# Batch 0's state products are stored and loaded ahead of the other batches', and one product changes place at the end of each pair

## The chip, the cores and the metric

The kernel runs on one core of one Trainium2 chip. The metric is the device time of one execution in microseconds (us), the median of several runs. Before the change it is 1326.22 us over 3 runs (1325.0 to 1326.81). Inside the core, TensorE (PE) multiplies matrices, VectorE (DVE), ScalarE (ACT) and GpSimd (POOL) work on elements, and SyncE (SP) issues most of the transfers between the on-chip memory and the chip's large memory (DRAM).

## The reference

Inputs are float32 or float64 arrays that the kernel takes as raw words where they are 64 bits wide. Three blocks follow one another:

```python
# attention: x is [8, 8, 512, 64], state is [8, 8, 32, 64] (batch, head, row, 64)
a     = softmax(x @ state.T / 8);   xread = a  @ state
a2    = softmax(state @ x.T / 8);   sread = a2 @ x
x     = concat([xread, sread], rows)              # per batch 512 + 32 rows
x     = x.transpose(0, 2, 1, 3).reshape(8 * 544, 512)

# block 1: w1, w2 [512, 1024], w3 [1024, 1024], w_out [1024, 512]
x     = ((x @ w1) * (x @ w2)) @ w3 @ w_out

# block 2: w_a, w_b [512, 1536], w_out [1536, 512]
out   = ((x @ w_a) * (x @ w_b)) @ w_out           # [4352, 512]
```

## The kernel before, in words

**How the work is arranged.** Every float32 product is made of three matrix multiplications on a high and a low part of each operand (`PASSES`, high x high, high x low, low x high). Block 1 does not form xread: since xread = a @ state, the kernel multiplies the state by w1 and w2 first. That gives one *state product* per batch, 256 rows by 2048 columns, and block 1 for the 512 x-rows of a batch is then (a @ product).

**The opening, up to about 180 us**, does four things at once: it converts and splits the weights, forms w3 @ w_out (tiles `wp`, then `ws`), runs the attention of batches 0 and 1, and makes the state products. A state product is made for four batches together: `state_product(p, nh, bg, i)` (L317) multiplies the state of head pair p of batches 4·bg to 4·bg+3 by half i of the column half nh of the weights `wk{p}_{nh}`. Two heads r give two PSUM banks `pb`. ACT or DVE copies them (`product_move`, L331) to a tile `sg{p}_{nh}_{bg}_{r}`, whose 128 rows are 4 batches by 32 state rows. `product_store` (L340) then writes the four 32-row parts to four DRAM buffers `p_d0` to `p_d3` (or `p_d4` to `p_d7` for bg = 1), one transfer each. There are 16 such tiles for each bg.

Before batch 0 can be multiplied, `load_p` (L597) loads its product back in four column chunks `pr0_0` to `pr0_3`, each over all rows. Chunks 0 and 1 need the stores with nh = 0, chunks 2 and 3 those with nh = 1. ACT casts a chunk to its high part `ph`, POOL subtracts to get the low part `pl` (`split`, L145 and L151). Two row chunks f of block 1 read one column chunk: `first_product` (L1107, its matmuls are at L1119, tiles `f0_*` and `f1_*`, 24 matmuls for the two f of a chunk), after which ACT and DVE make `fh`. When all eight `fh` exist, `first_output` (L1349, tiles `x2f0` to `x2f3`, 24 matmuls each) multiplies by `ws`. Batch 1 and the following batches run in a plain loop with tiles `ap`, `bp` and `x2p`.

**What sets the order of the opening.** Each piece of work is a `Job` with an engine, a planned duration, its predecessors (`after`), the number of free on-chip tiles it needs (`need`, plus `keep` that must stay free), a priority number and a `lag` after its predecessors. `run_jobs` (L724) always takes the job that could start first by its own clock, with the priority as a small handicap, or, among transfers, as the tie-breaker. What it picks becomes the order of instructions on each engine, and every engine then runs its own list strictly in this order. SP's list holds the stores and the loads together. The store of a tile is one job for all four batches, with priority `len(loads) + STORE_BEHIND`. The products of bg = 1 are jobs of low priority between the others.

**Block 2** works on pairs of batches g = 0 to 3 (`block2`, L1679) with a seven-product scheme in place of eight. For each row chunk f = 0 to 11 it does S2·T2 (into `r`, copied to `e2`), A12·B21 (into `q`), S4·B22 (added into `v`), S3·T3 (added into `r`), then the first two products of chunk f + 1, and then A22·T4 (added into `r`, L1756). Before A22·T4 may add into `r`, DVE must have added `r` into `e5` (`add`, L1583). For the last chunk, f = 11, there is no chunk f + 1, and A22·T4 stands directly behind S3·T3. After the twelve chunks, the results are multiplied by w_out (tiles `ro`, `vo`, `qo`).

Of the kernel before, what the change touches and what calls it, by code (L numbers as in the profile page):

```python
# [32 lines left out]
KEEP = 9  # L33
KEEP_SG = 2
KEEP_UNTIL = 40
STORE_BEHIND = 18

LATE_KEEP = 6
LATE_PRIO = 10
# [21 lines left out]
MARGIN = 1.5  # L61

P_AHEAD = 3
X_SLOT = 0
PASSES = ((0, 0), (0, 1), (1, 0))

# [2 lines left out]
def attention_moe_moe2(  # L69
# [18 lines left out]
    B, H, S, D = x.shape  # L88
# [10 lines left out]
    NF2 = DFF2 // P  # L99
# [16 lines left out]
    def charge(**work):  # L116
        for e, t in work.items():
            through[e] = max(through[e], now[0]) + t
        return max(through[e] for e in work)
# [43 lines left out]
    class Convert:  # L163
# [25 lines left out]
        def add(self, i):  # L189
            d, out = self.words(i)[1], self.out[:, i * 512 : (i + 1) * 512].bitcast(I32)  # L190
            nc.gpsimd.tensor_tensor(out=out, in0=out, in1=d.bitcast(I32), op=ALU.add)
            free(self.raws[i][0])
# [144 lines left out]
        else:  # L337
            nc.vector.tensor_copy(dst, src)

    def product_store(p, nh, bg, r):  # L340
        for j in range(4):
            nc.sync.dma_start(
                out=p_d[4 * bg + j][r, p, :, nh * 1024 : (nh + 1) * 1024],
                in_=sg[p, nh, bg, r][j * NS : (j + 1) * NS],
            )
# [330 lines left out]
    loads = []  # L676
# [53 lines left out]
            )  # L730
        return lows

    stores = {0: [], 1: []}

    def early_wk(p, nh):
        adds = convert_jobs(f"wk{p}_{nh}")
        last = []
        for bg in range(1):
            moves = {0: [], 1: []}
            for i in range(2):  # L740
                pr = Job(
                    "P",
                    1.0,
                    lambda a=(p, nh, bg, i): state_product(*a),
                    after=[adds[i], state_moved[bg]] + last[-1:],
                    need=2 - 2 * i,
                    keep=KEEP_SG,
                    prio=2 + len(loads) / 100,
                    banks=("ps", 2),
                )  # L750
                last.append(pr)
                for r in range(2):
                    moves[r].append(
                        Job(
                            "AV",
                            (0.6, 0.85),
                            lambda e, a=(p, nh, bg, i, r): product_move(*a, e),
                            after=[pr],
                            prio=0,
                        ).gives("ps", 1)  # L760
                    )
            for r in range(2):
                st = Job(
                    "D",
                    1.5,
                    lambda a=(p, nh, bg, r): product_store(*a),
                    after=moves[r],
                    prio=len(loads) + STORE_BEHIND,
                    lag=2.0,
                ).frees(f"sg{p}_{nh}_{bg}_{r}")  # L770
                if bg == 0:
                    stores[nh].append(st)
        return last

    def frees_after(after, *names):
# [47 lines left out]
    for name in EARLY:  # L823
        if name[:2] == "wk":
            p, nh = int(name[2]), int(name[4])
# [6 lines left out]
        elif name[:2] == "w3":  # L832
# [3 lines left out]
            for k in range(2):  # L836
# [4 lines left out]
                    after=list(adds),  # L841
                    prio=0,
# [6 lines left out]
                    after=[tr] + lows,  # L849
# [530 lines left out]
    for b, qs in ((0, range(4)), (1, range(3))):  # L1380
        for q in qs:
            l = Job(
                "D",
                1.5,
                lambda b=b, q=q: load_p(b, q),
                after=stores[q // 2] + ([last] if last else []),
                need=1,
                prio=1 + 20 * b,
                lag=1.0,
            )  # L1390
            if b == 0 or q == 0:
                sp = Job("A", 1.1, lambda b=b, q=q: split_p(b, q), after=[l], need=2, prio=0 + 5 * b)
                ready[b, q] = last = Job("G", 2.4, nothing, after=[sp], prio=0 + 5 * b)
    lows = []
    mults = []
    for f in range(NF1):
# [168 lines left out]
    def product(t, g, f, block, x, first):  # L1565
        for k in range(2):
            w = weights(g, f, block, k)
            for i, (m, q) in enumerate(PASSES):
                nc.tensor.matmul(  # L1569
                    t,  # L1570
                    lhsT=w[m],
                    rhs=xf[g].parts[x][q][:, k, :],
                    start=first and k == 0 and i == 0,
                    stop=k == 1 and i == 2,
                    skip_group_check=True,
                )
        now[0] += 6 * 512 / 2400 * 1.0625
# [101 lines left out]
    def block2(g):  # L1679
# [35 lines left out]
        def reload(f, i):  # L1715
            if g:
                free(f"w{g}_{f}_{i}")
                if f + 2 < NF2:
                    load_w(g, f + 2, [i])
# [4 lines left out]
        for f in range(NF2):  # L1724
# [7 lines left out]
            charge(A=0.6)  # L1732
            more()
            q = bank(f"q{name}")
            product(q, g, f, A12, "B21", True)
            reload(f, 1)
            add(e1, e1, q)
            charge(V=0.7)
            more()
            product(v, g, f, S4, "B22", False)  # L1740
            add(e2, e2, v)
            charge(V=0.7)
# [8 lines left out]
            h = [flat(out2.raw[f"{i + 1}{half}", j][1], S)[:, c, :] for i in range(2)]  # L1751
            nc.gpsimd.tensor_tensor(out=h[1], in0=e2, in1=e5, op=ALU.mult)  # L1752
            charge(G=1.3)
            if f + 1 < NF2:
                begin(f + 1)
            more()  # L1756
            product(r, g, f, A22, "T4", False)
            nc.vector.tensor_tensor(out=h[0], in0=e1, in1=r, op=ALU.mult)  # L1758
# [196 lines left out]
```

## Time and profile before

| | |
|---|---|
| median of 3 runs | 1326.22 us (1325.0 to 1326.81) |
| the profiled execution, its own time | 1323.77 us |
| span of the profile | 1322.0 us |
| PE busy | 1281.9 us, 97% of the span |
| DVE / ACT / POOL busy | 57% / 44% / 44% |
| granted TensorE clock, mean | 0.988 of full speed |

The profiled execution took 1323.77 us, 1.8 us more than its span; it is 2.45 us quicker than the median. PE is busy nearly all of the time, so a change shows in the end time mainly through what it does to the moments in which PE has nothing to do or runs at a lower clock. Busy shares of the other engines say little here: an idle engine that PE does not wait for costs nothing. Times in the rows count from the start of the span.

### The profile page before, as it was taken

Reading aid. Unit: us, or ns where it says so; the run is one execution under the profiler, and the core shown is the slowest. Engines: PE = TensorE matmul, PEld = TensorE weight load, DVE = VectorE, ACT = ScalarE, POOL = GpSimd, SP = SyncE. Lnnn points to the kernel's source line nnn. Section 1 sums busy time; section 2 is a strip of 40 time slices with the busy share of each in tenths; the row PEclk is TensorE's granted clock in tenths of the full one; section 3 lists DMA queues with packets and bytes.
Section 4 is the critical chain, followed back from the end, with each engine's and each line's share of the span. In section 5 each row is a group of like instructions: output and inputs, shape, how many; then the busy total and the mean of one; then the engine's idle time right before and its main releaser. Section 6 shows DMA issues by size and latency. Waiting matters only on the chain.

```text
span 1322.0 us, 19779 instructions
## 1 busy us (share of the span) xinstructions
PE 1281.9 (97%) x7514; PEld 1081.5 (82%) x7514; DVE 750.2 (57%) x861; ACT 585.5 (44%) x956; POOL 588.0 (44%) x398
## 2 busy tenths in 40 slices
PE   6996999999999999999999999999999999999998
PEld 4763778777777788888888998889988889988798
DVE  5883316557567566565665962247922359533493
ACT  7894535655565666545432431123511225212232
POOL 5671314563546567456447541147311264212460
PEclk7997999999999999999999999999999999999999
DMA  9988754762677561789584779316695247873271
GB/s 310 291 253 261 223 154 130 243 176 80 213 234 219 178 208 33 252 291 294 190 316 140 250 244 387 128 27 237 221 408 183 64 159 263 330 271 108 80 254 65
DMA packets 155134, 276.56 MB, mean 209 GB/s; under 512 B 47136, under 2 KB 92192, under 8 KB 155040
## 3 DMA queue, kind: packets, MB, share of 16 engines
q1 hardware_dynamic: 150752, 260.09, 59.5%
q0 software_dynamic: 4288, 15.21, 2.9%
q8 instruction: 60, 0.98, 0.3%
q14 instruction: 34, 0.28, 0.1%
HBM read 205.00 MB, written 70.25 MB: 208 GB/s over the span
## 4 chain that ended last, share of the span: by engine, by line
PE 86%; DMA 4%; DVE 3%; issue 2%; ACT 2%; SPq 1%; POOL 1%; POOLq 0%; ACTq 0%; DVEq 0%
PE r L1569 19%; PE ro L1887 10%; PE x2p L1178 10%; PE v L1569 9%; PE vo L1887 5%; PE bp L1119 5%; PE ap L1119 5%; PE q L1569 5%; PE qo L1887 3%; PE abs L1652 2%; PE f L1119 2%; PE x2f L1356 2%; PE wp L368 2%; PE srv L1826 1%; PE pb L324 1%
## 5 line engine op out<-in xcount | busy, mean ns | idle before, releaser
L1752 POOL TENSOR_TENSOR r<-e,e 128x512 f32<-128x512 f32 x48 | 63.5, 1324 | 283.9 <-DVE e L1583 283.9
L1178 PE MATMUL x2p<-hp,ws 128*128 128x512 f32 x672 | 162.0, 390 | 0.0
L151 POOL TENSOR_TENSOR pl<-pr,ph 128x512 fp32r<-128x512 f32 x64 | 87.4, 1385 | 137.3 <-ACT ph L145 104.8
L1178 PEld LDWEIGHTS x2p<-hp,ws 128*128 128x128 f32 x672 | 125.7, 188 | 26.3
L1703 ACT COPY e<-r 128x512 f32<-128x512 f32 x48 | 28.2, 588 | 188.7 <-PE r L1569 188.6
L1758 DVE TENSOR_TENSOR r<-e,r 128x512 f32<-128x512 f32 x48 | 33.0, 687 | 133.2 <-PE r L1569 133.2
L1143 DVE TENSOR_TENSOR hfp<-asbp,bp 128x512 f32<-128x512 f32 x56 | 38.3, 684 | 77.8 <-PE bp L1119 77.1
L151 DVE TENSOR_TENSOR hp<-hfp,hp 128x512 fp32r<-128x512 f32 x56 | 56.4, 1008 | 40.1 <-ACT hp L145 40.1
L1583 DVE TENSOR_TENSOR e<-e,q 128x512 f32<-128x512 f32 x48 | 32.9, 685 | 78.8 <-PE q L1569 78.8
L1607 POOL TENSOR_TENSOR r<-r,r 128x1024 f32<-128x1024 f32 x24 | 71.8, 3008 | 0.9
L1569 PE MATMUL r<-xT4h,w 128*128 128x512 f32 x192 | 67.8, 393 | 4.3 <-DVE e L1583 4.3
L1569 PE MATMUL r<-xT3h,w 128*128 128x512 f32 x192 | 67.1, 390 | 0.8 <-ACT e L1731 0.8
L1569 PE MATMUL r<-xT2h,w 128*128 128x512 f32 x192 | 67.1, 390 | 0.0
L1569 PE MATMUL r<-xB11h,w 128*128 128x512 f32 x192 | 67.0, 389 | 0.0
L1569 PE MATMUL q<-xB21h,w 128*128 128x512 f32 x192 | 66.9, 389 | 0.0
L1569 PE MATMUL v<-xB22h,w 128*128 128x512 f32 x192 | 66.9, 389 | 0.0
L1569 PE MATMUL v<-xT1h,w 128*128 128x512 f32 x192 | 66.9, 389 | 0.0
L145 ACT CAST hp<-hfp 128x512 fp32r<-128x512 f32 x56 | 34.8, 621 | 64.1 <-DVE hfp L1143 63.7
L1731 ACT COPY e<-r 128x512 f32<-128x512 f32 x48 | 28.3, 589 | 70.8 <-PE r L1569 70.8
L1137 ACT COPY asbp<-ap 128x512 f32<-128x512 f32 x56 | 32.8, 586 | 51.3 <-PE ap L1119 51.1
L1119 PE MATMUL bp<-ah,ph 128*128 128x512 f32 x112 | 48.0, 429 | 0.2 <-DVE hfp L1143 0.2
L1569 PEld LDWEIGHTS r<-xT4h,w 128*128 128x128 f32 x192 | 36.0, 188 | 14.6 <-DVE e L1583 7.2
(503 smaller groups left out, 3830.1 us busy)
## 6 DMA issues: line engine op xcount, KB each, us to landing
w<-w_d SPq DMA_DIRECT2D x132, 512.0 KB, 7.6
zz<-z_d SPq DMA_DIRECT2D x84, 512.0 KB, 4.5
w_d<-w SPq DMA_DIRECT2D x96, 256.0 KB, 3.2
p_d<-sg SPq DMA_DIRECT2D x128, 128.0 KB, 2.5
pr<-p_d SPq DMA_DIRECT2D x32, 512.0 KB, 5.8
w<-w_d SPq DMA_DIRECT2D x36, 256.0 KB, 8.4
x<-in_x_dram SPq DMA_DIRECT2D x64, 128.0 KB, 5.1
sw<-in_moe_w_dram SPq DMA_DIRECT2D x16, 512.0 KB, 5.2
```

What stands on the lines that cost most here:

```text
L145: nc.scalar.copy(hi, src)
L151: (eng or nc.vector).tensor_tensor(out=lo[:, i], in0=src[:, i], in1=hi[:, i].bitcast(F32), op=ALU.subtract)
L1119: nc.tensor.matmul(dst[:, :n], lhsT=l[m], rhs=r[q], start=i == 0 and j == 0, stop=i == k - 1 and j == 2,)
L1137: nc.scalar.copy(a_sb[:, :n], pa[:, :n])
L1143: nc.vector.tensor_tensor(out=hf[:, :n], in0=a_sb[:, :n], in1=pb[:, :n], op=ALU.mult)
L1178: nc.tensor.matmul(acc[j], lhsT=w_s[f][:, m, j * P : (j + 1) * P], rhs=h[:, q, :n], start=per == 1 and f == 0 and i == 0, stop=f == NF1 - ...
L1569: nc.tensor.matmul(t, lhsT=w[m], rhs=xf[g].parts[x][q][:, k, :], start=first and k == 0 and i == 0, stop=k == 1 and i == 2, skip_group_che ...
L1583: nc.vector.tensor_tensor(out=out, in0=x, in1=y, op=ALU.add)
L1607: ENGINES[eng].tensor_tensor(out=out, in0=x, in1=y, op=op)
L1752: nc.gpsimd.tensor_tensor(out=h[1], in0=e2, in1=e5, op=ALU.mult)
L1758: nc.vector.tensor_tensor(out=h[0], in0=e1, in1=r, op=ALU.mult)
L1887: nc.tensor.matmul(dst, lhsT=hl[m][:, k, i * P : (i + 1) * P], rhs=z[:, k, q, :], start=FIRST[p] and j == 0 and k == 0 and i % 2 == 0 and ...
```

## The change

It has two parts that do not touch each other.

**Stores and loads of batch 0.** The store of a bg = 0 tile is split in two jobs: the part of batch 0 with priority `len(loads) + STORE_FIRST` (6), and the parts of batches 1 to 3 behind it with `len(loads) + STORE_BEHIND` (now 40, before 18). The stores of bg = 1 stay one job each, with the latter priority. The loads of batch 0 wait for the first kind alone, the loads of batch 1 for the second. The loads of batch 0 are chained to one another, no longer to the split of the chunk before; they leave three tiles free (`P_KEEP`), and their planned lag grows from 1 to 4 us. The number of transfers, their sizes and all arithmetic stay as they were.

**The last row chunk of a pair.** For f = 11, A12·B21 with its addition on DVE moves from between S2·T2 and S4·B22 to between S3·T3 and A22·T4.

```diff
-STORE_BEHIND = 18
+STORE_FIRST = 6
+STORE_BEHIND = 40
...
+P_KEEP = 3
...
-    def product_store(p, nh, bg, r):
-        for j in range(4):
+    def product_store(p, nh, bg, r, js=range(4)):
+        for j in js:
             nc.sync.dma_start(
                 out=p_d[4 * bg + j][r, p, :, nh * 1024 : (nh + 1) * 1024],
                 in_=sg[p, nh, bg, r][j * NS : (j + 1) * NS],
...
-    stores = {0: [], 1: []}
+    stores = {(b, nh): [] for b in range(2) for nh in range(2)}
...
             for r in range(2):
                 st = Job(
                     "D",
+                    0.5,
+                    lambda a=(p, nh, bg, r, (0,)): product_store(*a),
+                    after=moves[r],
+                    prio=len(loads) + STORE_FIRST,
+                    lag=2.6,
+                )
+                rest = Job(
+                    "D",
                     1.5,
-                    lambda a=(p, nh, bg, r): product_store(*a),
-                    after=moves[r],
+                    lambda a=(p, nh, bg, r, (1, 2, 3)): product_store(*a),
+                    after=[*moves[r], st],
                     prio=len(loads) + STORE_BEHIND,
-                    lag=2.0,
+                    lag=2.6,
                 ).frees(f"sg{p}_{nh}_{bg}_{r}")
-                if bg == 0:
-                    stores[nh].append(st)
+                stores[0, nh].append(st)
+                stores[1, nh].append(rest)
...
                 lambda b=b, q=q: load_p(b, q),
-                after=stores[q // 2] + ([last] if last else []),
+                after=stores[b, q // 2] + ([last] if last else []),
                 need=1,
+                keep=P_KEEP,
                 prio=1 + 20 * b,
-                lag=1.0,
-            )
+                lag=4.0,
+            )
+            last = l if b == 0 else last
             if b == 0 or q == 0:
                 sp = Job("A", 1.1, lambda b=b, q=q: split_p(b, q), after=[l], need=2, prio=0 + 5 * b)
-                ready[b, q] = last = Job("G", 2.4, nothing, after=[sp], prio=0 + 5 * b)
+                ready[b, q] = Job("G", 2.4, nothing, after=[sp], prio=0 + 5 * b)
+            if q == (3, 0)[b]:
+                last = ready[b, q]
...
             q = bank(f"q{name}")
-            product(q, g, f, A12, "B21", True)
-            reload(f, 1)
-            add(e1, e1, q)
-            charge(V=0.7)
-            more()
+
+            def inner():
+                product(q, g, f, A12, "B21", True)
+                reload(f, 1)
+                add(e1, e1, q)
+                charge(V=0.7)
+                more()
+
+            last = f == NF2 - 1
+            if not last:
+                inner()
             product(v, g, f, S4, "B22", False)
...
-            if f + 1 < NF2:
+            if not last:
                 begin(f + 1)
+            else:
+                inner()
             more()
             product(r, g, f, A22, "T4", False)
```

**What moves on SP.** The stores of a tile end in its tile name and the batch is the number behind `p_d`; `pr0_0` is batch 0's first chunk. Around its load, before the change (56 stores stand ahead of the load):

```order
L342 DMA p_d2_85<-sg0_1_0_0_1037 32x1024
L342 DMA p_d3_86<-sg0_1_0_0_1037 32x1024
L342 DMA p_d0_83<-sg0_1_0_1_1040 32x1024
L342 DMA p_d1_84<-sg0_1_0_1_1040 32x1024
L342 DMA p_d2_85<-sg0_1_0_1_1040 32x1024
L342 DMA p_d3_86<-sg0_1_0_1_1040 32x1024
L600 DMA pr0_0_1204<-p_d0_83 128x2x512
L342 DMA p_d0_83<-sg3_1_0_0_1068 32x1024
```

And after it, on the same engine:

```order
L344 DMA p_d0_83<-sg2_0_0_0_1018 32x1024
L344 DMA p_d0_83<-sg2_0_0_1_1021 32x1024
L344 DMA p_d0_83<-sg0_1_0_0_1025 32x1024
L344 DMA p_d0_83<-sg0_1_0_1_1028 32x1024
L344 DMA p_d1_84<-sg0_0_0_1_942 32x1024
L344 DMA p_d2_85<-sg0_0_0_1_942 32x1024
L344 DMA p_d3_86<-sg0_0_0_1_942 32x1024
L344 DMA p_d1_84<-sg1_1_0_0_949 32x1024
L344 DMA p_d2_85<-sg1_1_0_0_949 32x1024
L344 DMA p_d3_86<-sg1_1_0_0_949 32x1024
L602 DMA pr0_0_1123<-p_d0_83 128x2x512
L344 DMA p_d0_83<-sg3_1_0_0_1055 32x1024
```

Now 29 stores stand ahead of the load: 14 of batch 0 and 15 of batches 1 to 3. The loads `pr0_1`, `pr0_2` and `pr0_3` follow with 8, 9 and 9 stores between each and the one before (16, 12 and 12 before the change). At the end of the opening, 40 stores of bg = 1 now stand in one piece between the loads `pr1_2` and `pr1_3` (24 before).

**What moves on PE.** `a2t1` is a transpose for batch 1's attention, `f0_0` batch 0's first product, `pb1_0_1_*` and `pb1_1_1_*` are state products of bg = 1. Before the change:

```order
L473 MATMUL a2t1_0_1211<-ident_78,e21_1200 128x128 x4
L473 MATMUL a2t1_1_1216<-ident_78,e21_1200 128x128 x4
L324 MATMUL pb1_0_1_0_0_1243<-wk1_0_731,stT_118 128x512
L324 MATMUL pb1_0_1_0_1_1246<-wk1_0_731,stT_118 128x512
L324 MATMUL pb1_0_1_1_0_1253<-wk1_0_731,stT_118 128x512
L324 MATMUL pb1_0_1_1_1_1255<-wk1_0_731,stT_118 128x512
L324 MATMUL pb1_1_1_0_0_1269<-wk1_1_770,stT_118 128x512
L324 MATMUL pb1_1_1_0_1_1272<-wk1_1_770,stT_118 128x512
L1119 MATMUL f0_0_1275<-ah0_661,ph0_0_1230 128x512
L1119 MATMUL f0_0_1275<-al0_662,ph0_0_1230 128x512
L1119 MATMUL f0_0_1275<-ah0_661,pl0_0_1231 128x512
```

After it:

```order
L326 MATMUL pb0_1_1_1_0_1194<-wk0_1_933,stT_118 128x512
L326 MATMUL pb0_1_1_1_1_1196<-wk0_1_933,stT_118 128x512
L475 MATMUL a2t1_0_1198<-ident_78,e21_1177 128x128 x4
L475 MATMUL a2t1_1_1203<-ident_78,e21_1177 128x128 x4
L1129 MATMUL f0_0_1224<-ah0_661,ph0_0_1189 128x512
L1129 MATMUL f0_0_1224<-al0_662,ph0_0_1189 128x512
L1129 MATMUL f0_0_1224<-ah0_661,pl0_0_1190 128x512
```

The six state products are gone from here, and so are those that stood between the groups of `f`: all 96 matmuls of `f` follow one another. The 24 state products of head pairs 1 to 3 come later: six behind the last `f`, two between `x2f1` and `x2f2`, sixteen behind `x2f3`, ahead of batch 1's first `ap`. The transpose `srt0` (batch 0's read of the state) moves ahead of the first two state products of bg = 1; before, it stood behind them. On ACT, the cast of `ph0_1` now stands ahead of the copies of `f0_0` and `f0_1` out of PSUM; before, it stood behind them.

**What moves on DVE at the end of a pair** (here pair 1; `q`, `v` and `r` are the PSUM banks, the last row is the split that follows). Before the change:

```order
L1583 TENSOR_TENSOR e_11_8538<-e_11_8538,q_11_8566 128x512
L1583 TENSOR_TENSOR e_11_8564<-e_11_8564,v_11_8540 128x512
L1583 TENSOR_TENSOR e_11_8547<-e_11_8547,r_11_8531 128x512
L1758 TENSOR_TENSOR r_12_2_8528<-e_11_8538,r_11_8531 128x512
L151 TENSOR_TENSOR r_11l_8597<-r_11_2_8130,r_11h_8596 128x1024
```

After it:

```order
L1597 TENSOR_TENSOR e_11_8564<-e_11_8564,v_11_8540 128x512
L1597 TENSOR_TENSOR e_11_8547<-e_11_8547,r_11_8531 128x512
L1597 TENSOR_TENSOR e_11_8538<-e_11_8538,q_11_8566 128x512
L1780 TENSOR_TENSOR r_12_2_8528<-e_11_8538,r_11_8531 128x512
L153 TENSOR_TENSOR r_11l_8597<-r_11_2_8130,r_11h_8596 128x1024
```

The addition of `q` moves behind that of `r`, as its product does on PE.

## Rows read from the trace of the kernel before

**Rows 1.** What PE waited for: us in total, times, longest us.

```profile
PE pb L324 <- ACT a L482: 11.3, 1, 11.3
...
PE r L1569 <- DVE e L1583: 4.3, 6, 1.0
```

**Rows 2.** Busy time of each engine by stretch, with PE's granted clock (PEclk).

```profile
100.00:110.00 10.00, 7.76 (x33) 3.23 (x29) 5.45 (x6) 5.22 (x14) 0.00 (x0) 1.00 0.89 254
...
120.00:130.00 10.00, 9.84 (x22) 6.10 (x23) 4.04 (x4) 6.38 (x13) 2.19 (x2) 0.57 0.89 272
```

**Rows 3.** The chain that ended last: start us, us, what.

```profile
113.11 5.45 DMA pr<-p_d
...
118.57 1.04 ACT ph L145
...
120.16 3.50 PE pb L324 x4
123.66 8.01 PE f L1119 x24
...
147.05 5.68 PE f L1119 x24
152.73 2.78 PE pb L324 x12
155.50 11.11 PE x2f L1356 x48
...
178.80 1.06 PE pb L324 x4
179.85 1.58 PE ap L1119 x6
```

**Rows 4.** SP's transfers in order: start us, us, what.

```profile
85.58 27.43 SPq L342 DMA_DIRECT2D p_d<-sg  x56
...
122.99 0.38 SPq L600 DMA_DIRECT2D pr<-p_d  x1
...
154.68 30.09 SPq L342 DMA_DIRECT2D p_d<-sg  x24
184.86 0.40 SPq L600 DMA_DIRECT2D pr<-p_d  x1
```

**Rows 5.** Transfers of the page: form, KB each, median us to landing.

```profile
p_d<-sg SPq DMA_DIRECT2D x128, 128.0 KB, 2.5
pr<-p_d SPq DMA_DIRECT2D x32, 512.0 KB, 5.8
```

**Rows 6.** DVE's last copy with nh = 0, in order of time.

```profile
94.76 0.69 DVE L338 COPY sg<-pb 128x512 f32<-128x512 f32 x1 [0.99 <-PE pb L324]
```

**Rows 7.** PE in order, 99 to 106 us.

```profile
99.61 1.13 PE L324 MATMUL pb<-wk,stT 64*128 64x512 f32 x4
101.80 0.33 PE L527 MATMUL srt<-ident,sn 128*128 128x128 f32 x1 [1.07 <-ACT sn L520]
...
104.84 1.09 PE L473 MATMUL a2t<-ident,e 128*128 128x128 f32 x8
```

**Rows 8.** ACT in order: the end of e21, and the chunk pr1_3.

```profile
105.03 0.19 ACT L440 ACTIVATION_READ_ACCUMULATOR e<-s,nm 128x1 f32 x1
...
206.25 1.05 ACT L145 CAST ph<-pr 128x1024 fp32r<-128x1024 f32 x1
```

**Rows 9.** POOL in order: the first low part.

```profile
119.70 2.49 POOL L151 TENSOR_TENSOR pl<-pr,ph 128x512 fp32r<-128x512 f32 x2 [25.11 <-ACT ph L145]
```

**Rows 10.** PE at the end of pair 3.

```profile
1254.32 0.39 PE L1569 MATMUL r<-xT3h,w 128*128 128x512 f32 x1
1255.49 0.50 PE L1569 MATMUL r<-xT4h,w 128*128 128x512 f32 x1 [0.78 <-DVE e L1583]
1255.83 0.40 PE L1569 MATMUL r<-xT4l,w 128*128 128x512 f32 x1
```

**Rows 11.** DVE and ACT at the end of pair 3.

```profile
1250.67 0.59 ACT L1731 COPY e<-r 128x512 f32<-128x512 f32 x1 [2.08 <-PE r L1569]
...
1254.74 0.69 DVE L1583 TENSOR_TENSOR e<-e,r 128x512 f32<-128x512 f32 x1 [0.57 <-PE r L1569]
```

## The prediction

> **What bounds the kernel now.** I read the views in this order: what PE waited for, busy time by stretch, the chain of waits across the opening, then SP, ACT and DVE around the two longest waits. PE is the engine to follow. Its longest wait is one of 11.3 us before a state product `pb`; the other entry of interest is 4.3 us in six waits of `r` for DVE's addition `e` [rows 1]. The first wait costs more than its idle time, because the clock falls with it: the granted clock is 1.00 in 100 to 110 us and 0.57 in 120 to 130 us [rows 2].
>
> The chain shows where the 11.3 us come from. The load of batch 0's first chunk is issued at 113.11, lands 5.45 us later, ACT casts it (1.04 us), copies once more, and only then PE goes on at 120.16 with a `pb` that needed a bank from ACT [rows 3]. The load waits for no data: it stands behind 56 stores that take SP 27.43 us from 85.58 on, 0.49 us each [rows 4], and 85.58 + 27.43 = 113.0. The last tile that chunks 0 and 1 need was complete at 94.76 + 0.69 = 95.45 [rows 6]. So the load is late by SP's queue alone, by some 14 us.
>
> **Part one, the load.** Now 29 stores stand ahead of it. At 0.49 us each, from 85.58 on, SP reaches the load at 85.58 + 14.2 = 99.8. Two other bounds are earlier: the last data at 95.45 plus seven stores is 98.9, and the landing of batch 0's last store, issued at about 96.4, is 98.9 with the median of 2.5 us [rows 5, 6]. I take 99.8. The chunk lands after 5.45 us, as in the chain (the median over all such loads, 5.8, gives 0.35 us more): 105.25. ACT is just done with `e21` at 105.22 [rows 8]. The cast ends at 106.3, POOL's two halves (2.49 us, [rows 9]) at 108.8.
>
> PE's side: it waits for `srt0` until 101.80 as now, but without the two state products (1.06 us by the four matmuls at 178.80) that filled the time before, so it idles 2.1 us where it idled 1.07 [rows 3, 7]. Then come eight state products, two more than now between `srt0` and `a2t`, which cost 4 x 2.78/12 = 0.93 us, so `a2t` moves from 104.84 to 105.8 and ends at 106.9 [rows 3, 7]. `f0_0` could start there; its last matmul needs POOL's second half at 108.8, so it ends at about 109.1 instead of 108.3. That is 0.8 us of new waiting in place of 11.3.
>
> From there PE's work is known. The four chunks of `f` at full clock take 5.68 us each; of 22.7 us the first `f0_0` (1.42) is done, so the end is at 109.1 + 21.3 = 130.4. Six state products, 2.78 us: 133.2. From the start of `x2f0` to the end of `x2f3` are 178.80 - 155.50 = 23.3 us, the two products between included: 156.5. The sixteen remaining products, 32 matmuls at 2.78/12, are 7.4 us: 163.9 for batch 1's first `ap`, now at 179.85 [rows 3]. Gain 15.9 us.
>
> The second way to this number is by what was lost. 11.3 us of idle time go. At the lower clock four matmuls of `pb` took 3.50 us, not 1.06, and 24 of `f` 8.01, not 5.68: 4.8 us more [rows 3]. Against it stand 1.0 us more before `srt0` and 0.8 us at `f0_0`: 11.3 + 4.8 - 1.8 = 14.3. The two ways differ by 1.6 us, which is about what scattered short stalls would take. I take 15.0, with 12 and 17 as ends.
>
> The cover of the moved state products: those that stood between the `f` groups filled time in which chunks were loaded. Now chunks must come every 5.68 us. SP has 8 or 9 stores and a load per chunk, about 9.5 x 0.49 = 4.7 us, so each is issued before PE needs it; ACT and POOL spend 1.04 and 2.49 us on it. At the end ACT copies sixteen results while PE makes them in 7.4 us; at 0.59 us for a copy of that size [rows 11] it needs 9.4 and ends up to 2 us after PE. Most of that lies beside the first `ap` and `bp`; what doesn't is in the step from 15.9 down to 15.0, and in the end of 12.
>
> SP's tail: 40 stores now stand ahead of `pr1_3`. The last 32 of them have data from about 158 on, and take 15.7 us, so the load goes out at about 174, 10 us after batch 1's start, where it was 5.0 us after (184.86 against 179.85). ACT casts that chunk 26.4 us after the start (206.25) [rows 3, 4, 8]. With 5.8 us to land, 10 us of cover remain: no cost. After that the order on all engines differs only in some pieces of weight intake, and PE is full, so the gain is carried to the end.
>
> **Part two, the pair's end.** Between the last two matmuls shown, PE loses: S3·T3's last starts at 1254.32, its successor at 1255.49, where one step is 5.68/24 = 0.23 us; 1.17 - 0.23 = 0.94, and the first step after the wait is 0.34 instead of 0.23. That makes 1.05 us, four times (the wait of 0.78 stands at the end of each of the four pairs) 4.2 us [rows 3, 10]. DVE sets it: it starts 0.19 us after PE's end, takes 0.69, and PE follows 0.06 later [rows 11]. Now A12·B21, six matmuls or 1.4 us, lies in the gap of 0.94: the gap is covered with 0.4 to 0.5 us to spare. What could be late next is S3·T3, which adds into `r` after ACT's copy `e2`. The copy starts at 1250.67, so S2·T2 ended at about 1250.5 (0.19 us earlier, as with DVE); it ends at 1251.26, and S3·T3 would now start one product behind S2·T2, at 1251.9: 0.6 us to spare. The addition of `q` is done while A22·T4 runs. I take 4.2 us; if the cover fails, 0.
>
> **Sum.** 15.0 + 4.2 = 19.2 us off the profiled execution's 1323.77 gives 1304.6. That execution is 2.45 us below the median of the runs, so on the medians' scale I predict 1307.0.
>
> **Rivals.** *The clock still falls.* PE's stops are now 2.1 us before `srt0` and 0.8 us at `f0_0`, near one another; the 1.07 us wait now leaves the clock at 1.00 in its stretch, the one of 11.3 does not [rows 1, 2, 7], and nothing between is shown. If it falls, the lower level costs what it cost, 4.8 us: 1311.8. [...]
>
> *The chunks pace PE, slower than before.* The first two loads of chunks are 9.9 us apart now (113.11 to 122.99, [rows 3, 4]). Without state products between them, PE would idle through the difference and run at the lower clock, where 24 matmuls take 24 x 0.43 = 10.3 us (0.43 is twice the 0.21 to 0.23 of the higher level). Four such chunks cost 4 x 4.6 = 18.5 us, which takes back 15.0 and nearly all of the pairs' 4.2. So the kernel is slower from a period of about 10.5 us on, and each further microsecond counts three times, once for each gap between chunks: at 13 us, 1326.2 - 19.2 + 18.5 + 8.1 = 1333.6. Against it: the 9.9 us were 16 stores and a load, now they are 8 and a load. For it: the cast of `ph0_1` now precedes the copies that free `f0_0`'s banks on ACT, and PE's wait of 11.3 us is already put down to an ACT copy behind the cast of a chunk [rows 1, 3]. [...]
>
> *Given back downstream.* The weight intake is planned anew behind the opening. If SP's tail or an intake makes PE wait in batches 1 to 3, half of part one could go: 1314.5. Against it: 10 us of cover at `pr1_3`.
>
> *The load doesn't move*, because it waits for stores behind which it no longer stands. Then only 4.2 us are left, 1322.0. Against it: the load's place behind 29 stores is a fact of the order.
>
> **Chances.** Forecast 0.70, lower clock 0.15, given back 0.08, load not moved 0.03, paced and slower 0.04. The range 1303.0 to 1314.0 has the upper end of part one (17 + 4.2, 1305.0, less the 1 to 2 us by which runs differ) at one side, and the lower clock with 2 us of other loss at the other. A measurement tells 0.2%, 2.7 us, from no change. Faster by more: 0.95; within: 0.02; slower: 0.03.
>
> **What would show it.** `pr0_0` issued near 100 us, `f0_0` running by 109, no wait over 2.5 us on PE between 95 and 165, batch 1's first `ap` at 163 to 166; the four 0.78 us waits gone. A `pr0_0` after 104, a granted clock below 0.9 in 110 to 130 us, or waits of `f` for POOL at each chunk would make the prediction wrong.

## The result, and the profile after

The changed kernel takes 1311.22 us (median of 5 runs, 1309.92 to 1311.8); the kernel before, run beside it, 1326.17 (1324.89 to 1326.81). That is 14.95 us less, a ratio of 0.9888 with a 95% interval of 0.9874 to 0.9903. The forecast was 1307.0, 19.2 us less, with 1303.0 to 1314.0 as range. The profiled execution took 1310.82 us (span 1309.0), 12.95 us less than that of before, which lay 2.4 us under the median of its five runs. All sums below are made between traces, so they are to be held against 12.95, not 14.95.

What PE waited for (us in total, times, longest), against [rows 1]:

```profile
PE srt L529 <- ACT sn L522: 3.7, 4, 2.1
PE f L1129 <- POOL pl L153: 2.2, 5, 1.2
PE r L1583 <- ACT e L1745: 2.0, 2, 1.7
PE ro L1909 <- DMA zz<-z_d: 1.4, 1, 1.4
...
PE f L1129 <- ACT sg L338: 1.2, 1, 1.2
PE r L1583 <- DVE e L1597: 1.2, 2, 1.0
PE qo L1909 <- DVE r_12l L153: 1.0, 1, 1.0
```

The wait of 11.3 us is gone, and so are the four of 0.78: `r` for DVE's `e` went from 4.3 us in six to 1.2 in two. New are `f` for POOL's `pl`, the longer wait of `r` for ACT's copy, and `qo` for `r_12l`. Of `srt`'s 3.7 us, 2.1 are the stop that the prediction counted. The windows that answer to [rows 2] (the last three numbers of a row are the clock, the DMA share and GB/s) show the full clock throughout:

```profile
100.00:110.00 10.00, 5.72 (x27) 2.75 (x27) 6.36 (x7) 6.87 (x16) 1.32 (x2) 1.00 0.82 250
110.00:120.00 10.00, 9.72 (x41) 7.63 (x42) 7.69 (x8) 7.13 (x13) 6.71 (x5) 1.00 0.84 287
120.00:130.00 10.00, 9.29 (x38) 6.50 (x38) 6.47 (x9) 5.70 (x11) 5.08 (x4) 1.00 0.84 251
```

SP's transfers, against [rows 4]:

```profile
85.62 15.17 SPq L344 DMA_DIRECT2D p_d<-sg  x29
100.89 0.39 SPq L602 DMA_DIRECT2D pr<-p_d  x1
101.39 5.39 SPq L344 DMA_DIRECT2D p_d<-sg  x8
106.88 0.45 SPq L602 DMA_DIRECT2D pr<-p_d  x1
107.38 6.22 SPq L344 DMA_DIRECT2D p_d<-sg  x9
113.71 0.38 SPq L602 DMA_DIRECT2D pr<-p_d  x1
114.13 5.73 SPq L344 DMA_DIRECT2D p_d<-sg  x9
120.12 0.38 SPq L602 DMA_DIRECT2D pr<-p_d  x1
```

The four chunk loads stand 6.0, 6.8 and 6.4 us apart; the prediction had 4.7. What ACT, POOL and PE did with the first chunk, one row of each engine, against [rows 7, 9]:

```profile
106.49 1.04 ACT L147 CAST ph<-pr 128x1024 fp32r<-128x1024 f32 x1 [0.68 <-DMA pr<-p_d]
```

```profile
108.68 2.51 POOL L153 TENSOR_TENSOR pl<-pr,ph 128x512 fp32r<-128x512 f32 x2 [14.01 <-DMA p_d<-sg]
```

```profile
110.01 0.50 PE L1129 MATMUL f<-ah,pl 128*128 128x512 f32 x1 [1.21 <-POOL pl L153]
```

POOL starts 1.2 us behind the cast's end (107.5), and a store released it. `pl0_0` got an on-chip tile that had held `sg1_1_0_1`, and that tile's stores of batches 1 to 3 now stand behind the load. The chain from there to batch 1, against [rows 3]:

```profile
129.39 4.60 PE f L1129 x19
134.00 2.78 PE pb L326 x12
136.77 11.11 PE x2f L1366 x48
...
160.06 7.07 PE pb L326 x32
167.13 1.60 PE ap L1129 x6
```

Batch 1's first `ap` starts 12.7 us before its old place (179.85). At the end of pair 3, PE's first matmul of S3·T3, of A12·B21 and of A22·T4, against [rows 10]:

```profile
1239.87 0.39 PE L1583 MATMUL r<-xT3h,w 128*128 128x512 f32 x1
...
1241.22 0.39 PE L1583 MATMUL q<-xB21h,w 128*128 128x512 f32 x1
...
1242.59 0.39 PE L1583 MATMUL r<-xT4h,w 128*128 128x512 f32 x1
```

The steps between are 1.35 and 1.37 us, six matmuls at 0.23, without a stop.

### The profile page after: what moved, and what is told of

It reads as the page before. It is cut to its first block, busy times and chain, and to the rows that moved or that the text cites. A ratio compares the mean times of both kernels' runs of the same rounds, so it can differ in the third digit from the quotient of the medians.

```text
span 1309.0 us, 19764 instructions
## 1 busy us (share of the span) xinstructions
PE 1275.8 (97%) x7514; PEld 1079.3 (82%) x7514; DVE 748.8 (57%) x861; ACT 584.4 (45%) x956; POOL 582.2 (44%) x398
## 4 chain that ended last, share of the span: by engine, by line
PE 81%; DVE 3%; ACT 2%; DMA 2%; issue 1%; POOL 1%; SPq 0%; ACTq 0%
PE r L1583 19%; PE ro L1909 10%; PE x2p L1188 10%; PE v L1583 9%; PE vo L1909 5%; PE bp L1129 5%; PE ap L1129 5%; PE q L1583 5%; PE qo L1909 2%; PE abs L1666 2%; PE x2f L1366 2%; PE srv L1848 1%; PE pb L326 1%; PE bs L1129 1%; DMA zr<-in_moe_w_out_dram 1%
## 5 line engine op out<-in xcount | busy, mean ns | idle before, releaser
L153 POOL TENSOR_TENSOR pl<-pr,ph 128x512 fp32r<-128x512 f32 x64 | 84.5, 1341 | 137.1 <-ACT ph L147 106.2
L1597 DVE TENSOR_TENSOR e<-e,v 128x512 f32<-128x512 f32 x48 | 32.9, 685 | 29.2 <-PE v L1583 22.8
```

The costliest lines, as they stand in the source:

```text
L153: (eng or nc.vector).tensor_tensor(out=lo[:, i], in0=src[:, i], in1=hi[:, i].bitcast(F32), op=ALU.subtract)
L1597: nc.vector.tensor_tensor(out=out, in0=x, in1=y, op=ALU.add)
```

## The experiments

### Part one alone

```diff
-            last = f == NF2 - 1
-            if not last:
-                inner()
+            product(q, g, f, A12, "B21", True)
...
-            else:
-                inner()
```

> Part one alone: the changed kernel with the old code at the end of the pairs. My theory: the two parts add up, and the pairs' part is worth 4 x 1.07 = 4.3 us (each pair's end came 1.07 us earlier in the changed kernel's trace). So this kernel stands 10.7 us below the kernel before (1315.5, ratio 0.992), and the four waits of 0.78 us of PE for DVE's e are there again. Rival: the pairs' part is worth less here, because PE would only wait elsewhere for work behind it: then the gain is 13 to 15 us (1311 to 1313). Second rival, against part one: the load's move alone gives what was forecast, 15 us, and the pairs' part nearly nothing.

Measured: 1313.24 us (1312.72 to 1315.7), before 1325.94; ratio 0.9907, 0.9894 to 0.9921. The gain is 12.7 us, between theory and rival. With the 3.5 of the next run the parts make 16.2 us, 1.2 more than the whole change, which their intervals allow. Part one is worth less than the 15 that I took.

### Part two alone

```diff
+            last = f == NF2 - 1
+            if not last:
+                inner()
...
+            else:
+                inner()
```

> Part two alone: the kernel before with the new order at the end of each pair. My theory: 4.2 us less than before (1322.0, ratio 0.9968), the four 0.78 us waits gone, the wait of 11.3 us untouched, the clock in 120 to 130 us still near 0.57. Rival: the time stays within 0.05% of before, because PE waits at the next place (S3T3 behind ACT's copy e2, or the first product of the next stage) for the same length.

Measured: 1322.45 us (1321.39 to 1326.01), before 1325.94; ratio 0.9978, 0.997 to 0.9987: 3.5 us. The four waits are gone, and there is a new one, once, at the end of pair 0:

```profile
PE qo L1895 <- DVE r_12l L151: 1.6, 1, 1.6
```

Neither the kernel before nor part one alone has this wait. So it belongs to part two, and the rival was right in kind, but for one pair out of four.

### Six stores between the chunk loads

```diff
-                lag=4.0,
+                lag=4.0 if q == 0 else 2.0,
```

> The changed kernel with 6 stores between the loads of batch 0's chunks 1, 2 and 3 where there are 9 (PE's order is the same). My theory: the three later chunks pace PE. A store takes SP 0.49 us because the transfer limits it, so a load of 512 KB counts like four stores; 9 + 4 at 0.49 are 6.4 us, over the 5.68 us that PE needs per chunk. With 6 stores the period is (6 + 4) x 0.49 = 4.9 us, and f ends about 2.0 us earlier (132.0 where it ended at 134.0): 1309.2, 0.15% less than the changed kernel. Rival: the copies on ACT, not the loads, set the pace of f; then f still ends at 134.0 and the time is the same within 0.5 us. Second rival: pr1_3 is now behind 48 stores; if its cover is used up, PE waits for it in batch 1.

Measured: 1311.54 us (1309.66 to 1312.44), ratio 0.9886, 0.9871 to 0.99: no gain. The loads came at 102.78, 108.62, 112.07 and 117.03, so those with six stores between were 3.45 and 4.96 us apart, and the five waits of `f` for `pl` became one. But the first load came 1.9 us later, behind the same 29 stores. ACT waited 2.45 us for a store before it could cast `ph0_1` into its tile, and the clock was 0.67 in 110 to 115 us. `f` ended at 134.72. Far behind the opening, after PE's wait of 1.8 us for ACT's copy in pair 0, the clock fell once more (0.83 in 670 to 680 us, where the changed kernel's was 1.00), which I put at 1.2 us. The trace is of the longest of the five runs. `pr1_3`, now behind 48 stores, made nobody wait. By itself the run settles nothing on the pace; the next ones take the disturbances away one at a time.

### The old order of the intake behind the opening

```diff
-    now[0] = clock["P"]
+    now[0] = 174.0
+    through.update(A=175.35, V=149.5, G=174.0, D=178.3)
+    when = [146.7] * 4 + ...
+    vacant[:] = [(t, u) for t, (_, u) in zip(when, sorted(vacant))]
```

> The changed kernel with the planner's clocks and tile times, behind the opening, set to those that the kernel before had there: the order of all engines behind the opening is then that of before, word for word, but for the pairs' ends. My theory: the 3.9 us that the changed kernel lost between batch 1's first ap (12.7 us earlier than before) and the first pairs (where it was 9.8 us earlier, without the 1.05 us of the pair's end) come from the new order of the weight intake in block 2's first pairs. Then this kernel is about 3.5 us below the changed one (1307.7). Rival: the loss comes from the times at which the weights arrive and not from the order (the loads are issued at the same moments or the same stores stand ahead); then it is the same within 1 us. Second rival: the old order, planned for a later end of the opening, is worse for the new one, up to 2 us slower.

Measured: 1315.59 us (1313.46 to 1320.13), ratio 0.9925, 0.9908 to 0.9942: 4.4 us slower than the changed kernel. My theory fell, and the second rival was right in sign, with more than its 2 us. PE waited 3.58 us for the attention of a later batch (`srt` at 194.85, for ACT's `sn`), and the clock fell behind that wait:

```profile
185.00:195.00 10.00, 6.42 (x59) 5.03 (x58) 1.86 (x4) 4.50 (x12) 0.96 (x1) 0.95 0.83 239
195.00:205.00 10.00, 10.00 (x37) 8.13 (x38) 6.76 (x9) 4.88 (x9) 3.83 (x3) 0.70 0.56 188
```

The trace is of the longest of the six runs, 4.5 us above their median, so this wait need not be as long in the others. But each of the six took longer than each of the changed kernel (1313.46 against 1311.8). An order planned for an end of the opening at another time is no neutral setting; the new plan was better here than the old one.

### The state's split one step later

```diff
             if g == 0 and j == 1:
...
-                if p < 6:
-                    so.split(p + 1, 0)
+            if g == 0 and j == (2 if p == 0 else 1) and p < 6:
+                so.split(p + 1, 0)
```

> The changed kernel, with the split of the state's second term (rs_12) one step later at the end of the first pair: on ACT and DVE it then stands behind the last split r_12 instead of ahead of it; nothing else moves. What it asks: why part two alone gave 3.5 us and not the 4.2 to 4.3 of four pair ends. My theory: at the end of pair 0 alone, DVE's subtraction r_11l takes 2.91 us in the new order where it took 1.41 in the old (POOL's additions lie beside it at another moment), and PE then waits 1.0 to 1.6 us for r_12l, which it did not before. With rs_12 behind r_12, r_12l ends 3 us earlier: the wait of qo for r_12l goes, 1.0 us off the changed kernel (1310.2), its waits otherwise the same. Rival: PE then waits as long for rs_12l, or the length of r_11l has nothing to do with it; then there is no difference within 0.3 us in the trace.

Measured: 1310.64 us (1309.14 to 1311.16), ratio 0.9878, 0.986 to 0.9896. On the time alone this could be no difference; the trace decides. The wait of `qo` is gone, and nothing took its place. DVE in the changed kernel:

```profile
703.24 2.91 DVE L153 TENSOR_TENSOR r_11l<-r,r_11h 128x1024 fp32r<-128x1024 f32 x1 [0.47 <-ACT r_11h L147]
...
708.59 6.21 DVE L153 TENSOR_TENSOR r_12l<-r,r_12h 128x1024 fp32r<-128x1024 f32 x2
714.72 3.17 DVE L153 TENSOR_TENSOR rs_12l<-rs,rs_12h 128x768 fp32r<-128x768 f32 x1
717.81 3.43 DVE L153 TENSOR_TENSOR r_12l<-r,r_12h 128x1024 fp32r<-128x1024 f32 x1
```

and in this one:

```profile
704.17 2.92 DVE L153 TENSOR_TENSOR r_11l<-r,r_11h 128x1024 fp32r<-128x1024 f32 x1 [0.46 <-ACT r_11h L147]
...
709.54 9.56 DVE L153 TENSOR_TENSOR r_12l<-r,r_12h 128x1024 fp32r<-128x1024 f32 x3
719.03 3.17 DVE L153 TENSOR_TENSOR rs_12l<-rs,rs_12h 128x768 fp32r<-128x768 f32 x1
```

The third `r_12l` ends at 721.2 in the first list and at 719.1 in the second, which as a whole lies 0.9 us later. So what delayed PE is DVE's list at this place, which begins with the long `r_11l`. It is as long here as there (2.92 us), so this run does not by itself show that its length is the cause.

### Two other tiles

```diff
-        hi, lo = unit(f"ph{b}_{q}", F32R), unit(f"pl{b}_{q}", F32R)
+        if (b, q) == (0, 1):
+            other_tile(2)
+        hi = unit(f"ph{b}_{q}", F32R)
+        if (b, q) == (0, 0):
+            other_tile(3)
+        lo = unit(f"pl{b}_{q}", F32R)
```

(`other_tile(k)` lets the next buffer change tiles with the k-th free one, whose planned time it keeps.)

> The changed kernel with other on-chip tiles for two buffers of the opening: pl0_0 and ph0_1 get tiles that held nothing with a store still to come (they held the score copy s1 and the weights wk0_1); before, they got tiles of sg1_1_0_1 and sg3_0_0_0, whose stores of batches 1 to 3 stand behind the load pr0_0 on SP. The order of all engines is unchanged. My theory: POOL's first subtraction then starts at the cast's end, 1.2 us earlier, and the cast of ph0_1 1 us earlier (the chunk's landing then ends that wait), but the later chunks arrive when they did, each 6 to 6.8 us behind the one before, so f still ends near 134.0 and the time is the same within 0.5 us. Rival: the loss of part one against its forecast came from these two tiles; then f ends 1 to 1.2 us earlier and so does the kernel (1310.1).

Measured: 1309.92 us (1309.4 to 1310.8), ratio 0.9876, 0.9861 to 0.989. The median fits the rival better than my "the same within 0.5", though the ranges of both kernels' runs overlap. POOL's wait for a store is gone, and PE's for `pl` in this stretch fell from 2.2 to 0.5 us. `f` ended at 133.03, with the first load at 101.77 and the last at 119.25.

### Six stores and the two tiles

```diff
-                lag=4.0,
+                lag=4.0 if q == 0 else 2.0,
...
+            other_tile(2)
...
+            other_tile(3)
```

> Both edits of the opening together: 6 stores between the loads of chunks 1, 2 and 3, and the two other tiles. My theory: of SP's transfers, the eighth behind a load waits until the load has landed (SP waited for pr<-p_d 6.2 us in 4 waits in the changed kernel), so with 8 or 9 stores between, a chunk can't come faster than it lands; with 6 stores the next load is issued before that. With the tiles no wait for stores is left on ACT and POOL. Then f runs without waits from about 109 to 110 on, ends at 131 to 132, and batch 1's first ap starts at 164 to 165.5 (167.13 in the changed kernel, 167.85 with the six stores alone): 2 us less, 1309.2. Rival: the six-store run gained nothing because the first load itself came later (102.78 where it was 100.89, behind the same 29 stores) or because the clock fell in 110 to 115 us (0.67); if these come again, f ends at 134 again.

Measured: 1309.42 us (1308.39 to 1309.92), ratio 0.987, 0.9855 to 0.9885. SP's transfers:

```profile
102.49 0.39 SPq L602 DMA_DIRECT2D pr<-p_d  x1
102.99 4.65 SPq L344 DMA_DIRECT2D p_d<-sg  x8
107.73 0.38 SPq L602 DMA_DIRECT2D pr<-p_d  x1
108.16 3.15 SPq L344 DMA_DIRECT2D p_d<-sg  x6
111.41 0.38 SPq L602 DMA_DIRECT2D pr<-p_d  x1
112.48 2.91 SPq L344 DMA_DIRECT2D p_d<-sg  x6
115.44 0.43 SPq L602 DMA_DIRECT2D pr<-p_d  x1
```

The later loads are 3.7 and 4.0 us apart. A load that cost as much as four stores would put them (6 + 4) x 0.49 = 4.9 us apart, as I had written for the six stores; that picture is wrong. `f` ended at 132.67 and `ap` began at 165.81, though the first load came 1.6 us later than in the changed kernel. In time the run can't be told from the two tiles alone (1309.92): the ranges overlap, and in this trace PE stood 2.0 us at `ro`, where it stood 1.4 in the changed kernel.

### All three

```diff
-                lag=4.0,
+                lag=4.0 if q == 0 else 2.0,
...
+            other_tile(2)
...
+            other_tile(3)
...
+            if g == 0 and j == (2 if p == 0 else 1) and p < 6:
+                so.split(p + 1, 0)
```

> The changed kernel with all three: six stores between the loads, the two tiles, and the split of rs_12 one step later. My theory: the gains add up, 2 us of the opening and 1 us at the end of pair 0, less what the first pairs give back because ACT waits there for weights that come at their own pace (PE waited 1.7 us for ACT's copy e at 670 us, 0.8 before): 1308.5, with 1307.5 to 1310.0 as ends. Rival: all of the opening's further gain is given back in block 2's first pair; then only 1.0 is left, 1310.2.

Measured: 1308.31 us (1307.81 to 1309.02), ratio 0.9863, 0.9849 to 0.9878. This beats both kernels: none of its runs is as slow as the fastest of the changed kernel (1309.92). The gain of 2.9 us is close to the 2.7 that were expected.

### The first load from POOL's queue

```diff
-        nc.sync.dma_start(out=flat(t, 512), ...)
+        (nc.gpsimd if (b, q) == (0, 0) else nc.sync).dma_start(...)
```

> The kernel of the run before (all three edits), with the one load pr0_0 issued from POOL's queue instead of SP's; all else in the same order. What it asks: the first load was forecast at 99.8 us (29 stores at 0.49) and came at 100.9 to 102.8 in six traces, 15.2 to 16.9 us behind the same 29 stores. My theory: it still waits for SP's queue alone. The last store that it needs goes out near 97 and lands 2.5 to 3 us later; POOL has nothing to do from 95.6 on, so the load is issued near 100 at the latest, lands at 105.5, and f's first subtraction and all behind it come 2 us earlier: batch 1's first ap near 164.9 (166.91 in the trace of all three), 1306.5 in time. Rival: the load itself lands later when it goes out amid the stores (16 engines were 80 to 90% busy there), or a load from POOL's queue costs over 1 us more to issue; then the chunk lands at 107 or later and the time is that of all three, 1308.3, within 0.5 us.

Measured: 1308.65 us (1307.33 to 1309.82), ratio 0.9865, 0.9849 to 0.9882: by time not to be told from all three. In its trace the load went out where I expected it:

```profile
99.87 0.91 POOL L602 DMA_DIRECT2D pr<-p_d  x1 [4.76 <-DMA p_d<-sg]
```

It landed 6.0 us later, the cast began at 106.77, straight behind `e21`, and `ap` began at 165.02 (expected 164.9). On SP the same load went out at 100.89 to 102.78. This shows that SP's queue alone held the first load there; what it is worth in time stays open.

### PE held back behind the opening

```diff
+    for i in range(8):
+        hold = bank(f"hold{i}")
+        for _ in range(7):
+            nc.tensor.matmul(hold, lhsT=warm[:, :P], rhs=warm, start=True, stop=True)
```

> The changed kernel with PE held back by about 12 us behind the opening: 56 matmuls whose result nothing reads, in eight banks, directly ahead of batch 1's first ap; no other engine's order moves. What it asks: between batch 1's first ap and the end of block 2's first pair the changed kernel gave back 2.2 us of its 12.7 (12.66 ahead of before at the first ap, 10.42 ahead at the last r of pair 0). My theory: there weights come at the pace of the transfers (the 16 engines are full from 570 us on, PE waited for w<-w_d, and 1.7 us for an ACT copy behind a weight that came late), so a PE that arrives 12 us later finds them ready: the hold costs 2 us less at that point than it did at the first ap, and the time is about 1321 (1311.2 + 12 - 2). Rival: the loss is one of the order of the intake as planned, or of noise; then all of the hold is still there at the end of pair 0 and the time is 1323 or more.

Measured: 1322.66 us (1321.56 to 1324.21), ratio 0.9974, 0.9965 to 0.9983. The time lies between theory and rival; the trace tells more. PE at the same place of pair 0, S3·T3 behind ACT's copy `e2`, in the kernel before, the changed one and this one:

```profile
681.07 0.50 PE L1569 MATMUL r<-xT3h,w 128*128 128x512 f32 x1 [0.83 <-ACT e L1731]
```

```profile
670.59 0.50 PE L1583 MATMUL r<-xT3h,w 128*128 128x512 f32 x1 [1.73 <-ACT e L1745]
```

```profile
681.45 0.50 PE L1587 MATMUL r<-xT3h,w 128*128 128x512 f32 x1 [0.21 <-ACT e L1749]
```

At the first `ap` the hold is 12.39 us (its first matmul starts at 179.45, in the changed kernel at 167.06); here 10.86 are left. The 1.5 us between are the shorter wait, 1.73 to 0.21. In the changed kernel ACT had stood 4.12 us in front of this copy, at the conversion of a weight that had not landed; here 2.58:

```profile
665.07 0.67 ACT L178 ACTIVATE zr<-zr 128x512 f32<-128x512 f32 x1 [4.12 <-DMA zr<-in_moe_w_out_dram]
```

```profile
675.89 0.67 ACT L178 ACTIVATE zr<-zr 128x512 f32<-128x512 f32 x1 [2.58 <-DMA zr<-in_moe_w_out_dram]
```

SP issued the loads of this weight here, in the changed kernel and in this one:

```profile
656.07 0.87 SPq L162 DMA_DIRECT2D zr<-in_moe_w_out_dram  x2
```

```profile
668.52 0.90 SPq L162 DMA_DIRECT2D zr<-in_moe_w_out_dram  x2
```

They moved with PE by the whole hold, 12.45 us. So the weight does not have a time of its own, as my theory had it; what differs is the time from the issue to ACT's conversion, 9.0 us in the changed kernel and 7.4 here. It was 8.0 in the kernel before, where ACT's stop was 3.20 us and PE waited 0.83; in part two alone these were 3.63 and 1.28. In these four traces PE's wait is longer where ACT's stop is. Why the weight takes longer stays open, and since part two alone has the opening of before, some of the difference is scatter.

## Why the prediction was right, and where its sizes were off

The mechanism was right on both parts, and the time lay in the range. The size of the gain was too large: by traces 12.95 us in place of 19.2, by medians 14.95. Nearly every term that was off was off to the same side. Two of the prediction's own signs went against it: batch 1's first `ap` came at 167.13, not at 163 to 166, and `f` waited for POOL at three of the four chunks, though behind the first chunk for only 0.7 us in all. Part one's steps:

| step | predicted | trace |
|---|---|---|
| load `pr0_0` issued | 99.8 | 100.89 |
| cast ends | 106.3 | 107.5 |
| POOL's two halves end | 108.8 | 111.2 |
| `f` ends | 130.4 | 134.00 |
| six `pb`, the `x2f` and their `pb` end | 156.5 | 160.06 |
| first `ap` | 163.9, taken as 164.9 | 167.13 |

*29 stores at 0.49 us.* They took 15.17 us, not 14.2, and between 15.81 and 16.75 in seven other traces with the same list (part one alone, six stores, the old intake, the state's split later, the two tiles, six stores and the tiles, all three), with the load at 101.8 to 102.8; the result's trace has the earliest load of them. The 0.49 was a mean over the old order, to which nothing bound the new one. This term was 1.1 us too small in the trace of the result, and up to 3 in others.

*POOL follows the cast.* It waited 1.2 us for a store that the change itself had put behind the load. The prediction counted which stores stand ahead of the load, but not who waits for those behind it.

*Chunks every 4.7 us.* They came every 6.0 to 6.8, over the 5.68 that PE needs (5.0 to 6.9 in the other traces with eight and nine stores between). In the program nearly every transfer of SP waits for the one eight before it (710 of the 726 that have one), as the instruction list shows for the first load and the eighth transfer behind it (the same semaphore comes round):

```
97 L602 DMA pr_0_1123<-p_d_83 128x2x512 [waits DMAHW5_49,Pool_49]
...
105 L344 DMA p_d_86<-sg_0_0_0_974 32x1024 [waits DMAHW5_49]
```

The four chunk loads took 5.4 to 5.9 us to land, 5.5 in the median, and SP stopped in the stores behind each of them until it had landed:

```profile
SPq L344 <- DMA pr<-p_d: 6.2, 4, 2.0
```

So with eight or nine stores between, each load here went out only after the one before had landed, 6.0 to 6.8 us behind it. With six stores between, the loads were 3.5 to 5.0 us apart in the four traces that have them. From the first load's issue to the first `ap` the changed kernel needs 66.2 us, and 65.2 to 66.0 in the other runs with this opening that go straight on to `ap` (part one alone, the old intake, the state's split later). With the two tiles alone it is 64.4, with six stores and the tiles 63.3 and, in all three, 64.2. So SP's waits show what held the chunks, but what six stores add to the tiles is too small to be priced. The rival "chunks pace PE" was thus half true. It named the right place, but the period was 6.0 to 6.8 us, not 10.5, and its cost was about 1.1 us (`f` took 22.4 us behind `f0_0`, predicted 21.3). The 0.43 us of that rival's slow matmul is in the trace of the kernel before: `f`'s matmuls between 124.2 and 128.4 us start 0.43 us apart at a clock of 0.50 (122 to 128 us), and 0.23 apart at 1.00 (130 to 132 us).

*The rest of the opening* came out as counted: 26.06 us from the end of `f` to the end of the last `x2f` against 26.1, and 7.07 against 7.4 for the sixteen products.

*The clock.* In the result's trace it did not fall, as the forecast's 1307.0 had it, but that was luck. Of nine traces with the moved load, all but the hold's, it stayed at 1.00 between 100 and 115 us only in this one and with six stores and two tiles. In the other seven it fell to between 0.66 and 0.80 in at least one stretch of 5 us there, and three of these have the same opening (0.80 in part one alone, 0.69 with the old intake and with the state's split later). Where the chunks set the pace this cost little, as the 65.2 to 66.0 us above show against 66.2. So the measured 1311.22 is nearer to the rival "the clock still falls" (1311.8) than to the forecast, but in the trace that rival's 4.8 us were not lost.

*Nothing late downstream.* This step, "the gain is carried to the end", failed. From the first `ap` (12.72 us ahead) to S3·T3 of pair 0 (10.48 ahead) 2.24 us were given back. Up to 404 us it is 0.3, as short waits came and went. The rest is three stops in pair 0, the one of 1.73 us above and two before it that the kernel before does not have:

```profile
568.42 0.47 PE L1583 MATMUL r<-xB11h,w 128*128 128x512 f32 x1 [0.23 <-DMA w<-w_d]
...
580.10 0.50 PE L1583 MATMUL r<-xT3h,w 128*128 128x512 f32 x1 [0.23 <-ACT e L1745]
```

These two cost 1.1 us together. They come again with the hold (1.0 us), where PE arrives when it did in the kernel before, and the old intake has two such stops nearby (0.95 us). So neither PE's earlier arrival nor the new order is shown as their cause; it stays open. The third costs 0.9 us more than before by ACT's wait for the weight, and in the hold it is nearly gone. The rival "given back downstream" had half of part one at stake; it was a sixth.

*Part two.* The gap is covered as counted, 1.07 us at the ends where nothing follows. The step that failed is "four times": at pair 0 it is lost again, since PE then waits for `r_12l` (1.03 us here, 0.8 to 1.6 in six of the seven traces with this list of splits; in the seventh, with six stores and two tiles, PE had already lost as much at `ro`). The prediction looked at S3·T3 and at the addition of `q`, not at the splits that DVE makes behind the pair's end. There `r_11l` takes 2.91 us where it took 1.41, and `rs_12l` 3.17 where it took 2.60, so the last `r_12l` ends 2.1 us later behind DVE's last addition of the pair. That this is why PE waits follows from the durations; no run changed them alone. DVE's `r_11l` before, and POOL's addition beside it before and after:

```profile
714.78 1.41 DVE L151 TENSOR_TENSOR r_11l<-r,r_11h 128x1024 fp32r<-128x1024 f32 x1 [0.47 <-ACT r_11h L145]
```

```profile
715.07 2.80 POOL L1607 TENSOR_TENSOR rs_S<-rs,rs 128x768 f32<-128x768 f32 x1
```

```profile
703.23 1.84 POOL L1621 TENSOR_TENSOR rs_S<-rs,rs 128x768 f32<-128x768 f32 x1
```

In the kernel before DVE's `r_11l` took 1.41, and POOL, 0.29 us behind, took 2.80. In the changed one POOL began at 703.23, 0.01 us ahead of DVE, and took 1.84, and DVE took 2.91 (0.01 us says little by itself, but the durations differ by far more). Part two alone has 2.92 on DVE and 1.85 on POOL; part one alone, with the old end of a pair, has 1.39 and 2.80. On DVE the run with the state's split later has 2.92, the one with all three 2.91. In these pairs the one that is recorded first has the shorter of its two durations, and the other took 0.96 us (POOL) or 1.50 us (DVE) longer. Why is not shown, and it is no full measure of `r_11l`, which took from 1.41 to 3.42 us at its twelve places in the kernel before.

*The sum by the traces.* 12.72 us at the first `ap`, less 2.24 up to pair 0. At the end of pair 0 1.07 us came and 1.7 went: 0.4 at `ro`, which waited 1.4 us for `z_d` where it waited 1.0, and the rest at `qo`. The three other ends gave 3.2. That is 13.0, the difference of the spans (1322.0 and 1309.0). The forecast's 19.2 were 15.0 and 4.2.

## What to carry to other kernels

When stores are put behind a load, ask twice: what the load no longer waits for, and who now waits for what was put back, through the tile that a late store keeps. Count a queue's issue rate with the transfers that are outstanding in it: in this program, where nearly every transfer of SP waits for the one eight before it, SP stood 6.2 us in four waits for 512 KB loads among 128 KB stores. And a gain of microseconds early in a kernel need not arrive whole at its end: here 2.2 of 12.7 us went in short stops, most of them 400 to 500 us later. Holding the main engine back by the same time shows which of these stops it meets even then.

## What the runs showed of the hardware

The same 29 stores in the same order took from 15.17 to 16.75 us from one trace to the next, in eight traces, and the load behind them went out at 100.89 to 102.78. At the end of pair 0 an addition on POOL (`rs_S`) and a subtraction on DVE (`r_11l`) began within 0.3 us of each other and took 2.80 and 1.41 us with DVE recorded 0.29 us ahead, 1.84 and 2.91 with POOL 0.01 us ahead. Which of the two came first changed with a product's place a few microseconds before, and DVE's subtraction took 1.50 us longer.
